# Attention into a mixture of experts: the order of scaling, routing and first expert slices behind the last chunks

## The chip, the cores and the metric

One core of one Trainium2 chip runs the whole kernel. Its engines work side by side, each on its own list of instructions in order: TensorE (PE in the rows; its weight loads are PEld), VectorE (DVE), ScalarE (ACT), GpSimd (POOL) and SyncE (SP, which here only issues DMAs). The metric is the device time of one execution in microseconds (us); less is better.

## The reference

Windowed attention with a linear bias, whose output rows are the tokens of a mixture of experts with one expert per token:

```python
# B, H, S, D = 8, 8, 576, 64; window 128
scores = scale * q @ k^T + slopes * (-|rel|), masked to 0 <= rel < 128
x = softmax(scores) @ v            # -> (4608, 512): N tokens, DM = 512
# E = 8 experts, F = 1024
logits = x @ w_gate
expert_idx = argmax(logits); gate_w = softmax(logits)[expert_idx]
out[mask_e] = gate_w * (relu(x[mask_e] @ w1[e]) @ w2[e])
```

## The kernel before

**Attention** runs over 36 chunks of 128 tokens. For each chunk TensorE makes scores (tile s_ps), VectorE masks them and takes the maximum (nmax), ScalarE takes the exponentials (pe) with their sums, TensorE transposes (t_ps), ScalarE copies the transposes (pT), GpSimd masks them, TensorE multiplies with v (x_ps), and the function rows makes from that the rows in token order, with the gate's logits in 16 more columns of each of four parts: tile r_ps, one buffer in PSUM. VectorE then scales r_ps by 1/sum into x_sb, in two instructions: the logit columns (128x64 elements) and the rows (128x512). The function done, called behind that, sums the logits into lg and has SyncE store the rows to xd in DRAM.

**Routing.** Groups of chunks (GROUPS) go through route, a generator of five stages: one-hot of the chosen expert (oh); rank of each token in its expert, by products with the triangle tri, and the gates; rank within a tile of 128 as a mask lp, and column numbers c; the products rr of an equality mask eq with the token numbers; and the index products lp x rr, added into base, the table from which the rows are gathered later. Rank and index products go into the spare columns of r_ps, from step 146 on into t_ps. route_last does the same for chunk 35 alone, with names that begin with l_, and ends with idx, the table of the first expert's late rows.

**The order is written by hand**: 152 steps, four to a chunk, and each engine's list follows the order in which step calls things. PACE says at which steps a late group takes its next stage. The last full group holds chunks 30 to 34; its first stage runs at step 149, where the rows of chunk 34 are made; those of chunk 35 are made at step 151. To keep TensorE at work, early computes the first layer of seven slices of the first expert for 256 rows that are known by then (e_xh, e_xl to s_ps to e_hh, e_hl; 12 products each, two buffers of s_ps). EP gives the step of each of these slices (0 to 2), LE the slices that route_last puts between its parts (3 to 6). Behind that a scheduler orders the expert layers: first layer2 of the seven early slices, then the rows gathered by idx, and so on.

Of the kernel before, what the change touches and what calls it, by code (L numbers as in the profile page):

```python
# [36 lines left out]
def attention(ctx, tc, st, qT, kT, v, c1, cb, iw, load_c2, chunk_done, chunks, begun):  # L37
# [163 lines left out]
    def rows(ch, subs, xT, rsum):  # L201
        rinv = small.tile([128, H], F32, name="rinv")
        nc.vector.reciprocal(out=rinv, in_=rsum)
        st["r_ps"] = r_ps = ps_r.tile([128, NP, 256], F32, name="r_ps")
        for p in range(NP):
            nc.tensor.matmul(out=r_ps[:, p, 0:XW], lhsT=xT[:, p, :], rhs=iw_sb[:, p, :], start=True, stop=True)  # L206
        x_sb = xp.tile([128, NP, XW], F32, name="x_sb")
        for lo, n in ((128, E), (0, D)):
            cols = slice(lo, lo + 2 * n)
            split = lambda ap: ap[:, :, cols].rearrange("q p (c x) -> q p c x", c=2)  # L210
            nc.vector.tensor_tensor(  # L211
                out=split(x_sb), in0=split(r_ps),
                in1=rinv.rearrange("q (p c) -> q p c", c=2).unsqueeze(3).to_broadcast([128, NP, 2, n]), op=ALU.mult)
        chunk_done(ch, subs, x_sb)
# [54 lines left out]
    def step(s):  # L269
# [21 lines left out]
        if s in EP:  # L291
            early(EP[s])

# [40 lines left out]
LW = (0, 0, 0, 0)  # L334
# [7 lines left out]
EP = {60: "z", 134: "g", 143: "p0", 146: "p1", 147: "0", 149: "1", 150: "2"}  # L342
LE = ("3", "4", "56", "")
# [49 lines left out]
def route(tc, st, lg, c0, G, groups):  # L393
# [65 lines left out]
    for k, n in enumerate(("tokh", "tokl")):  # L459
        nc.vector.tensor_tensor(out=rr[:, :, k, :], in0=eq,  # L460
# [36 lines left out]
def route_last(tc, st, lg, ch, groups):  # L497
# [23 lines left out]
    for r in st["rest"]:  # L521
        next(r)
        next(r)
    st["warm"](1)
# [11 lines left out]
    ip = st["ps_x"].tile([128, 512], F32, name="x_ps")[:, 0:E * TT]
    t0 = EARLY // 128
    for t in range(t0, TT):
        lp = rp.tile([128, 128], BF16, name=f"l_lp{t}", bufs=1)
        nc.vector.tensor_scalar(out=lp, in0=st["i128"], scalar1=s, scalar2=-128.0 * t, op0=ALU.subtract,  # L540
                                op1=ALU.is_equal)
        for k in range(2):
            nc.tensor.matmul(out=ip[:, E * t:E * t + E], lhsT=lp, rhs=rr[:, k, :], start=(k == 0), stop=(k == 1))
# [7 lines left out]
    st["warm"](3)  # L551
# [126 lines left out]
def moe_static(ctx, tc, st, w12, out):  # L678
# [26 lines left out]
    def gather(p, t, behind=None):  # L705
# [7 lines left out]
        else:  # L713
            xg[p, t] = gather_rows(tc, st, g, column(p, t))
# [344 lines left out]
def attn_moe_kernel(ctx, tc, qT, kT, v, c1, cb, c2, iw, w12, out):  # L1059
# [9 lines left out]
    with ExitStack() as actx:  # L1069
# [9 lines left out]
        def done(ch, subs, x_sb):  # L1079
# [7 lines left out]
            for lo in (0, 2):  # L1087
                if lo == 2 and subs[0][0] == subs[2][0]:
                    continue
                n = 64 if subs[0][0] != subs[2][0] else 128  # L1090
                t0 = subs[lo][0] * S + QB * subs[lo][1]
                nc.sync.dma_start(out=st["xd"][t0:t0 + n].rearrange("t (p x) -> t p x", p=NP),
                                  in_=x_sb[QB * lo:QB * lo + n, :, 0:SUB])
# [67 lines left out]
```

## Time and profile before

| | |
|---|---|
| time, median of 3 runs (lowest, highest) | 672.54 us (672.29, 672.86) |
| the profiled execution: its time, its span | 674.61 us, 672.8 us |
| PE busy | 647.7 us (96%) |
| DVE, ACT, POOL busy | 398.6, 313.1, 309.2 us |

The span is the time from the first to the last instruction; 1.8 us lie around it. Busy PE is not PE at its peak, since products overlap and their ends are modelled; what counts here is where it is idle, and what ended that.

### The profile page before, as it was taken

To read this page: it belongs to the slowest core of one execution; us is meant where nothing else is said; L and a number is where in the kernel's file an instruction comes from. 1 tells how busy PE (TensorE), PEld (TensorE's weight loads), DVE (VectorE), ACT (ScalarE), POOL (GpSimd) and SP (SyncE) were. 2 spreads that over 40 slices of the span, in tenths; PEclk is the share of its full clock that TensorE was granted. 3 is DMA by queue.
4 is the path that set the end of the run, shared out by engine and by line. 5 is a ranking of instruction groups with operands and counts; after the bars stand their busy time and mean duration, and the time that the engine had idled before them with its cause. 6 is when DMAs were issued, how large, how long until landed. Compare 5 with 4: busy or idle time off the path is not lost.

```text
span 672.8 us, 15622 instructions
## 1 busy us (share of the span) xinstructions
PE 647.7 (96%) x5937; PEld 551.2 (82%) x5937; DVE 398.6 (59%) x976; ACT 313.1 (47%) x940; POOL 309.2 (46%) x425
## 2 busy tenths in 40 slices
PE   7899999999999989999999999999999999999995
PEld 3688787787787878999988988989898989888884
DVE  3468878877888777553555355365456455456411
ACT  3777778887776511442234234233434333333311
POOL 2546567786654413016524751860762560471202
PEclk8999999999999999999999999999999999999999
DMA  9477696795853316335323442532543542453201
GB/s 319 131 199 182 177 248 164 256 261 133 264 144 82 94 34 189 111 117 170 93 81 109 144 128 82 181 106 85 173 107 109 174 114 77 159 147 111 89 0 59
DMA packets 55360, 94.24 MB, mean 140 GB/s; under 512 B 11622, under 2 KB 31334, under 8 KB 54386
## 3 DMA queue, kind: packets, MB, share of 16 engines
q1 hardware_dynamic: 46882, 73.18, 37.2%
q0 software_dynamic: 8400, 20.02, 10.4%
q8 instruction: 48, 0.79, 0.5%
q14 instruction: 30, 0.25, 0.1%
HBM read 74.20 MB, written 18.97 MB: 138 GB/s over the span
## 4 chain that ended last, share of the span: by engine, by line
PE 51%; issue 8%; POOL 3%; DMA 1%; DVE 1%; ACT 1%; POOLq 0%; ACTq 0%
PE y_ps L762 24%; PE l_ps L634 23%; POOL xg L614 2%; POOL out L749 1%; PE x_ps L762 1%; PE s_ps L634 1%; PE x_ps L596 1%; DMA xd<-x_sb 1%; PE x_ps L196 1%; DMA xg<-xd,idx 0%; PE r_ps L206 0%; DMA out<-y,od_pidx 0%; DVE x_sb L211 0%; ACT pe L159 0%; POOLq L812 0%
## 5 line engine op out<-in xcount | busy, mean ns | idle before, releaser
L637 DVE SCALAR_TENSOR_TENSOR hl<-l_ps,hh 128x334 fp32r<-128x334 f32 (+7 forms) x104 | 52.7, 506 | 162.5 <-ACT hh L636 162.4
L636 ACT ACTIVATE hh<-l_ps 128x334 fp32r<-128x334 f32 (+7 forms) x104 | 46.9, 451 | 216.4 <-PE l_ps L634 216.1
L614 POOL DMA_INDIRECT xg<-xd,od_idx x112 | 114.8, 1025 | 35.8 <-issue 35.2
L159 ACT ACTIVATE pe<-s_ps,nmax 128x128 f32<-128x128 f32 x288 | 102.2, 371 | 48.9 <-DVE nmax L155 39.8
L762 PE MATMUL y_ps<-wh,hh 128*128 128x512 f32 (+2 forms) x288 | 114.2, 397 | 0.0
L762 PE MATMUL y_ps<-wl,hh 128*128 128x512 f32 (+2 forms) x288 | 113.6, 394 | 0.0
L762 PE MATMUL y_ps<-wh,hl 128*128 128x512 f32 (+2 forms) x288 | 113.5, 394 | 0.0
L749 POOL DMA_INDIRECT out<-y,od_pidx x34 | 36.3, 1068 | 153.7 <-ACT y L768 147.2
L852 DVE TENSOR_TENSOR wl<-w_raw,wh 128x512 fp32r<-128x512 f32 x114 | 73.9, 689 | 23.2 <-ACT wh L848 22.1
L634 PE MATMUL l_ps<-xh,wl 128*128 128x304 f32 (+9 forms) x416 | 80.8, 316 | 0.0
L634 PE MATMUL l_ps<-xh,wh 128*128 128x304 f32 (+9 forms) x416 | 80.7, 316 | 0.0
L634 PE MATMUL l_ps<-xl,wh 128*128 128x304 f32 (+9 forms) x416 | 80.6, 316 | 0.0
L634 PEld LDWEIGHTS l_ps<-xh,wh 128*128 128x128 f32 x416 | 68.3, 189 | 7.4
L634 PEld LDWEIGHTS l_ps<-xh,wl 128*128 128x128 f32 x416 | 66.1, 189 | 2.0
L634 PEld LDWEIGHTS l_ps<-xl,wh 128*128 128x128 f32 x416 | 66.0, 189 | 1.9
L196 PE MATMUL x_ps<-pT,v_sb 128*64 128x128 f32 (+2 forms) x1152 | 66.4, 265 | 0.1
L762 PEld LDWEIGHTS y_ps<-wh,hl 128*128 128x128 f32 (+2 forms) x288 | 53.0, 184 | 13.9
L196 PEld LDWEIGHTS x_ps<-pT,v_sb 128*64 128x64 f32 (+1 forms) x1152 | 57.0, 137 | 7.8 <-issue 2.8
L762 PEld LDWEIGHTS y_ps<-wl,hh 128*128 128x128 f32 (+2 forms) x288 | 53.1, 184 | 11.6
L762 PEld LDWEIGHTS y_ps<-wh,hh 128*128 128x128 f32 (+2 forms) x288 | 53.0, 184 | 10.8 <-ACT hh L636 0.4
L159 ACT ACTIVATION_READ_ACCUMULATOR pe<-s_ps,nmax 128x1 f32 x288 | 60.2, 209 | 0.0
L138 PE MATMUL s_ps<-k_sb,q_sb 64*64 64x192 f32 (+2 forms) x1152 | 57.3, 307 | 2.6 <-DMA k_sb<-kT 2.6
(207 smaller groups left out, 980.6 us busy)
## 6 DMA issues: line engine op xcount, KB each, us to landing
w_raw<-w SPq DMA_DIRECT2D x64, 512.0 KB, 3.7
q_sb<-qT SPq DMA_DIRECT2D x40, 256.0 KB, 7.1
xd<-x_sb SPq DMA_DIRECT2D x32, 258.0 KB, 4.9
v_sb<-v SPq DMA_DIRECT2D x32, 256.0 KB, 4.9
k_sb<-kT SPq DMA_DIRECT2D x7, 1152.0 KB, 8.3
xg<-xd,od_idx POOLq DMA_INDIRECT x112, 3.2
xd<-x_sb SPq DMA_DIRECT2D x8, 129.0 KB, 4.2
v_sb<-v SPq DMA_DIRECT2D x8, 128.0 KB, 4.7
```

The source lines that it names most:

```text
L138: nc.tensor.matmul(out=s_ps[halves(a), c, n, x0:x1], lhsT=blocks["q", b, m][h, 2 * g + n, qs], rhs=batch[b][h, 2 * g + n, k0:k0 + x1 - x0] ...
L159: nc.scalar.activation(out=pe[:, h, :], in_=s_ps[:, c, n, lo:lo + 128], func=AF.Exp, bias=nmax[:, 2 * c + n:2 * c + n + 1], scale=1.0, acc ...
L196: nc.tensor.matmul(out=x_ps[64 * c:64 * c + 64, p, q], lhsT=blocks["v", b, m - 1 + kb][0:kk, D * h:D * h + D], rhs=pT[0:kk, kb, h, q], sta ...
L596: nc.tensor.transpose(out=x_ps[:, d, :], in_=g[:, SUB * d:SUB * d + 128], identity=st["ident"])
L614: ins = tc.nc.gpsimd.indirect_dma_start(out=g[:, s], out_offset=None, in_=parts, in_offset=bass.IndirectOffsetOnAxis(ap=idx[:, s], axis=0),)
L634: nc.tensor.matmul(out=ps, lhsT=a[:, 128 * d:128 * d + 128], rhs=b[:, d], start=(k == 0), stop=(k == 11))
L636: nc.scalar.activation(out=hh, in_=ps, func=AF.Relu)
L637: nc.vector.scalar_tensor_tensor(out=hl, in0=ps, scalar=0.0, in1=hh.bitcast(F32), op0=ALU.max, op1=ALU.subtract)
L749: ins = nc.gpsimd.indirect_dma_start(**kw).ins
L762: nc.tensor.matmul(out=ys[t][0:m], lhsT=a[:, tl], rhs=b[:, 512:1024], start=(f == 0 and k == 0), stop=(f == 7 and k == 2))
L852: keep(tc, eng.tensor_tensor(out=wl[:, sl], in0=raw[:, sl], in1=wh.bitcast(F32)[:, sl], op=ALU.subtract))
```

## The change

Five things change.

- The two scalings of a chunk are split: the logit columns are scaled, then lg is summed, then the rows are scaled and stored. For chunks 0 to 33 that is the same place with another order. For chunk 34 scaling and store of the rows wait until the route stage of step 149 is written, for chunk 35 until the rank products of route_last.
- PACE and the step function let a stage be taken twice in a step: the last full group takes two stages at step 150, where it took one, and one in route_last ahead of its index products, where it took two behind the rank.
- Slice 2 moves from step 150 to 149, so that slices 1 and 2 stand in front of the group's rank products. route_last places 3, then 4 and 5, then 6, instead of 3, then 4, then 5 and 6.
- In route_last rank, gate and masks (l_lp) of chunk 35 come first, then the group's fourth stage, then the index products of chunk 35, then those of the group. One of the last full group's two rr products (tokh) moves to GpSimd.
- The gathers of the first expert's late rows and six memsets of hh and hl are held in program order: gathers first.

```diff
@@ rows
-        for lo, n in ((128, E), (0, D)):
+        def scale(lo, n):
...
-        chunk_done(ch, subs, x_sb)
+        scale(128, E)
+        chunk_done(ch, subs, x_sb, lambda: scale(0, D))
@@ step
-            if k[1] <= s and (s in PACE[k[2]] if k[2] in PACE else s % 4 == 2):
+            if k[1] <= s:
                 k[1] = s + 1
-                if next(k[0], k) is k:
-                    st["stages"].remove(k)
+                for _ in range(PACE[k[2]].count(s) if k[2] in PACE else s % 4 == 2):
+                    if next(k[0], k) is k:
+                        st["stages"].remove(k)
+        if "store" in st:
+            st.pop("store")()
@@ tables
-PACE = {21: (122, 126, 130, 132, 134), 27: (138, 142, 144, 146, 148), 30: (149, 150)}
+PACE = {21: (122, 126, 130, 132, 134), 27: (138, 142, 144, 146, 148), 30: (149, 150, 150)}
-EP = {60: "z", 134: "g", 143: "p0", 146: "p1", 147: "0", 149: "1", 150: "2"}
-LE = ("3", "4", "56", "")
+EP = {60: ("z",), 134: ("g",), 143: ("p0",), 146: ("p1",), 147: "0", 149: "12"}
+LE = ("3", "45", "6")
@@ route
-        nc.vector.tensor_tensor(out=rr[:, :, k, :], in0=eq,
+        eng = nc.gpsimd if c0 + G == N // 128 - 1 and k == 0 else nc.vector
+        eng.tensor_tensor(out=rr[:, :, k, :], in0=eq,
@@ route_last
-    for r in st["rest"]:
-        next(r)
-        next(r)
-    st["warm"](1)
+    st.pop("store")()
...
     put_gates(tc, st, gate, groups)
+    t0 = EARLY // 128
+    lps = {}
+    for t in range(t0, TT):
+        lps[t] = rp.tile([128, 128], BF16, name=f"l_lp{t}", bufs=1)
+        nc.vector.tensor_scalar(out=lps[t], in0=st["i128"], scalar1=s, scalar2=-128.0 * t, op0=ALU.subtract,
+                                op1=ALU.is_equal)
+    st["warm"](1)
+    for r in st["rest"]:
+        next(r)
     st["warm"](2)
+    ip = st["ps_x"].tile([128, 512], F32, name="x_ps")[:, 0:E * TT]
+    for t in range(t0, TT):
+        for k in range(2):
+            nc.tensor.matmul(out=ip[:, E * t:E * t + E], lhsT=lps[t], rhs=rr[:, k, :], start=(k == 0), stop=(k == 1))
     for r in st["rest"]:
         list(r)
@@ moe_static
-            xg[p, t] = gather_rows(tc, st, g, column(p, t))
+            xg[p, t] = gather_rows(tc, st, g, column(p, t), held=p == 0)
...
-            nc.gpsimd.memset(a[:, min(CAPS):].bitcast(F32), 0.0)
+            keep(tc, nc.gpsimd.memset(a[:, min(CAPS):].bitcast(F32), 0.0))
@@ done
-            for lo in (0, 2):
...
+            def store():
+                scale()
...
+            if ch < N // 128 - 2:
+                store()
+            else:
+                st["store"] = store
```

VectorE behind the rows of an ordinary chunk, before: both scalings (x_sb), then the sum (lg), then the next scores.

```order
L203 RECIPROCAL rinv<-rsum 128x8
L211 TENSOR_TENSOR x_sb<-r_ps,rinv 128x4x16
L211 TENSOR_TENSOR x_sb<-r_ps,rinv 128x4x128
L1085 TENSOR_REDUCE lg<-x_sb 128x8
L152 COPY_PREDICATED s_ps<-c_sb,s_ps 128x4x128
L155 TENSOR_REDUCE nmax<-s_ps 128x4
```

The same place now:

```order
L203 RECIPROCAL rinv<-rsum 128x8
L212 TENSOR_TENSOR x_sb<-r_ps,rinv 128x4x16
L1095 TENSOR_REDUCE lg<-x_sb 128x8
L212 TENSOR_TENSOR x_sb<-r_ps,rinv 128x4x128
L152 COPY_PREDICATED s_ps<-c_sb,s_ps 128x4x128
L155 TENSOR_REDUCE nmax<-s_ps 128x4
```

The sum stands between the two scalings; so it is at every chunk from 0 to 33.

VectorE at steps 150 and 151, before: the end of the last full group's rank (rank, t), a slice's e_hl, and chunk 35 from 1/sum (rinv) to its one-hot.

```order
L433 TENSOR_REDUCE rank<-pick 128x5
L435 TENSOR_SCALAR t<-rank 128x5
L436 TENSOR_SCALAR t<-t 128x5
L637 SCALAR_TENSOR_TENSOR e_hl<-s_ps,e_hh 128x256
L203 RECIPROCAL rinv<-rsum 128x8
L211 TENSOR_TENSOR x_sb<-r_ps,rinv 128x4x16
L211 TENSOR_TENSOR x_sb<-r_ps,rinv 128x4x128
L1085 TENSOR_REDUCE lg<-x_sb 128x8
L503 CAST l_prev<-run 128x8
L505 TENSOR_REDUCE l_mx<-lg 128x1
L507 SCALAR_TENSOR_TENSOR l_key<-lg,l_mx,c_sb 128x8
L508 TENSOR_SCALAR l_mx<-l_mx 128x1
```

The same place now:

```order
L439 TENSOR_REDUCE rank<-pick 128x5
L441 TENSOR_SCALAR t<-rank 128x5
L442 TENSOR_SCALAR t<-t 128x5
L450 SCALAR_TENSOR_TENSOR p<-t,rank 128x5
L452 TENSOR_TENSOR lp<-c_sb,p 128x640
L455 TENSOR_SCALAR c<-mk 128x5
L457 TENSOR_SCALAR big<-rank 128x5
L203 RECIPROCAL rinv<-rsum 128x8
L212 TENSOR_TENSOR x_sb<-r_ps,rinv 128x4x16
L1095 TENSOR_REDUCE lg<-x_sb 128x8
L510 CAST l_prev<-run 128x8
L512 TENSOR_REDUCE l_mx<-lg 128x1
```

The group's third stage (p, lp, c, big) stands ahead of chunk 35's scaling, the slice's e_hl has gone ahead of the rank, and the scaling of chunk 35's rows behind its one-hot.

TensorE at steps 149 and 150, before: slice 1 (with the numbers that tell the slices apart), then the rank of the last full group.

```order
L634 MATMUL s_ps_4430<-e_xh_68,wh_1983 128x256 x4
L634 MATMUL s_ps_4430<-e_xh_68,wl_1984 128x256 x4
L634 MATMUL s_ps_4430<-e_xl_69,wh_1983 128x256 x4
L419 LDWEIGHTS tri_148
L419 MATMUL t_ps_4447<-oh_4426,tri_148 128x40
```

The same place now:

```order
L644 MATMUL s_ps_4430<-e_xh_68,wh_1983 128x256 x4
L644 MATMUL s_ps_4430<-e_xh_68,wl_1984 128x256 x4
L644 MATMUL s_ps_4430<-e_xl_69,wh_1983 128x256 x4
L644 MATMUL s_ps_4447<-e_xh_68,wh_2218 128x256 x4
L644 MATMUL s_ps_4447<-e_xh_68,wl_2219 128x256 x4
L644 MATMUL s_ps_4447<-e_xl_69,wh_2218 128x256 x4
L425 LDWEIGHTS tri_148
L425 MATMUL t_ps_4464<-oh_4424,tri_148 128x40
```

Slice 2 stands between slice 1 and the rank.

## Rows read from the trace of the kernel before

**Rows 1.** Busy time of each engine in two stretches, with the number of instructions, the granted TensorE clock, the DMA share and GB/s: the change from attention to the experts (235 to 262 us), and the expert layers behind it.

```profile
235.00:262.00 27.00, 23.86 (x173) 20.67 (x172) 19.66 (x98) 5.03 (x14) 7.90 (x13) 1.00 0.36 105
...
262.00:640.00 378.00, 378.00 (x2067) 333.74 (x2067) 197.17 (x425) 133.50 (x212) 160.76 (x178) 1.00 0.40 121
```

**Rows 2.** TensorE in order of time at four of the products that write into the spare columns of r_ps (start us, length us, line, operation; in brackets the idle time before it and what ended it).

```profile
62.85 0.18 PE L419 MATMUL r_ps<-oh,tri 128*128 128x40 bf16 x1 [0.41 <-DVE x_sb L211]
...
81.14 0.41 PE L466 MATMUL r_ps<-rr,lp 128*128 128x48 bf16 x10 [0.88 <-DVE x_sb L211]
...
211.16 0.46 PE L466 MATMUL r_ps<-rr,lp 128*128 128x48 bf16 x12 [1.18 <-DVE x_sb L211]
...
222.24 0.17 PE L419 MATMUL r_ps<-oh,tri 128*128 128x24 bf16 x1
```

**Rows 3.** VectorE in order of time at the third of these: the two scalings of a chunk (merged in one row), the sum of its logits, and the next instruction.

```profile
210.28 0.82 DVE L211 TENSOR_TENSOR x_sb<-r_ps,rinv 128x64 f32<-128x64 f32 x2
211.02 0.26 DVE L1085 TENSOR_REDUCE lg<-x_sb 128x8 f32<-128x64 f32 x1
211.19 0.69 DVE L152 COPY_PREDICATED s_ps<-c_sb,s_ps 128x512 f32<-128x512 uint32 x1
```

**Rows 4.** VectorE, instructions grouped by line and shape: busy us in all, mean ns of one.

```profile
L211 DVE TENSOR_TENSOR x_sb<-r_ps,rinv 128x512 f32<-128x512 f32 x36 | 24.5, 680 | 0.0
...
L211 DVE TENSOR_TENSOR x_sb<-r_ps,rinv 128x64 f32<-128x64 f32 x36 | 8.1, 225 | 4.5 <-PE r_ps L206 1.5
```

**Rows 5.** VectorE and TensorE in order of time, rows with idle time in front of them: where VectorE waited for the score products, and TensorE for the copies of the transposed weights.

```profile
84.53 0.43 DVE L152 COPY_PREDICATED s_ps<-c_sb,s_ps 128x256 f32<-128x256 uint32 x1 [1.83 <-PE s_ps L138]
...
130.40 0.70 DVE L152 COPY_PREDICATED s_ps<-c_sb,s_ps 128x512 f32<-128x512 uint32 x1 [0.38 <-PE s_ps L138]
...
166.96 0.70 DVE L152 COPY_PREDICATED s_ps<-c_sb,s_ps 128x512 f32<-128x512 uint32 x1 [0.33 <-PE s_ps L138]
...
213.86 0.70 DVE L152 COPY_PREDICATED s_ps<-c_sb,s_ps 128x512 f32<-128x512 uint32 x1 [0.94 <-PE s_ps L138]
...
226.83 0.66 PE L168 MATMUL t_ps<-c_sb,pe 128*128 128x128 f32 x4 [0.44 <-ACT pT L170]
```

**Rows 6.** TensorE in order of time, 237 to 255 us: products of ranks (L419, L519), slices of the first expert layer (L634), products with the second layer (L762), index products (L466), transposes of gathered rows (L596).

```profile
237.96 0.18 PE L419 MATMUL t_ps<-oh,tri 128*128 128x40 bf16 x1 [0.84 <-DVE oh L413]
...
238.17 0.72 PE L634 MATMUL s_ps<-e_xh,wh 128*128 128x256 f32 x4
...
239.68 1.14 PE L206 MATMUL r_ps<-iw_sb,xT 128*128 128x144 f32 x8
...
242.89 0.17 PE L519 MATMUL x_ps<-l_oh,tri 128*128 128x8 bf16 x1 [0.64 <-DVE l_oh L515]
...
246.60 0.75 PE L634 MATMUL s_ps<-e_xh,wh 128*128 128x256 f32 x4 [0.57 <-DVE e_hl L637]
...
249.45 0.47 PE L762 MATMUL y_ps<-wh,e_hh 128*128 128x512 f32 x1 [0.87 <-DVE base L468]
...
250.63 0.48 PE L762 MATMUL y_ps<-wh,e_hh 128*128 128x512 f32 x1
...
250.94 0.39 PE L762 MATMUL y_ps<-wl,e_hh 128*128 128x512 f32 x1
...
251.17 0.40 PE L762 MATMUL y_ps<-wh,e_hl 128*128 128x512 f32 x1
...
254.67 0.66 PE L596 MATMUL x_ps<-c_sb,xg 128*128 128x128 f32 x4 [0.21 <-DMA xg<-xd,idx]
```

**Rows 7.** VectorE in order of time, 235 to 245 us.

```profile
235.73 0.82 DVE L211 TENSOR_TENSOR x_sb<-r_ps,rinv 128x64 f32<-128x64 f32 x2 [0.75 <-PE r_ps L206]
...
236.78 0.20 DVE L402 TENSOR_REDUCE mx<-lg 128x5 f32<-128x40 f32 x1
...
238.35 0.20 DVE L425 TENSOR_TENSOR pick<-t_ps,oh 128x40 f32<-128x40 f32 x1
...
240.29 0.42 DVE L637 SCALAR_TENSOR_TENSOR e_hl<-s_ps,e_hh 128x256 fp32r<-128x256 f32 x1 [0.39 <-ACT e_hh L636]
...
240.63 0.19 DVE L203 RECIPROCAL rinv<-rsum 128x8 f32<-128x8 f32 x1
...
242.61 0.23 DVE L515 TENSOR_SCALAR l_oh<-l_key,mk 128x8 bf16<-128x8 f32 x1
...
243.51 0.16 DVE L444 SCALAR_TENSOR_TENSOR p<-t,rank 128x5 f32<-128x5 f32 x1
...
244.64 0.17 DVE L453 TENSOR_TENSOR c<-c,t 128x5 f32<-128x5 f32 x1
```

**Rows 8.** Instructions grouped by line and shape: a product of two tiles on GpSimd, and on VectorE the one of two that the change moves to GpSimd (busy us in all, mean ns of one).

```profile
L869 POOL TENSOR_TENSOR wl<-w_raw,wh 128x512 fp32r<-128x512 f32 x14 | 18.5, 1322 | 3.5 <-ACT wh L864 3.4
...
L460 DVE TENSOR_TENSOR rr<-eq,c_sb 128x240 bf16<-128x240 f32 x8 | 3.2, 442 | 0.1
```

**Rows 9.** DMA issues from the page: tiles, queue, operation, number, KB in all, median us from issue to landing.

```profile
xd<-x_sb SPq DMA_DIRECT2D x32, 258.0 KB, 4.9
```

**Rows 10.** TensorE at the wait near the start, and busy time of each engine in two stretches behind it, with the granted clock (columns as in Rows 1).

```profile
8.19 0.67 PE L138 MATMUL s_ps<-k_sb,q_sb 64*64 64x64 f32 x16 [2.56 <-DMA k_sb<-kT]
...
9.00:10.00 1.00, 0.94 (x10) 0.17 (x12) 0.96 (x2) 0.00 (x0) 0.17 (x1) 0.50 1.07 382
...
12.00:13.00 1.00, 1.00 (x21) 0.71 (x24) 0.59 (x1) 0.31 (x2) 0.00 (x0) 0.81 1.11 446
```

More of the change, by code (lines that the diff above doesn't have):

```diff
@@ L290, in step @@
             st["load"]((s - FETCH + 12) // 8)
-        if s in EP:
-            early(EP[s])
+        for op in EP.get(s, ()):
+            early(op)
     with tc.manual_schedule(engines=HANDS(nc)):
@@ L333 @@
 RB = 2
-LW = (0, 0, 0, 0)
+LW = (0, 0, 0)
 FREE_T = 146
 WU = (9, 1, 1, 1, 1, 1, 2, 2, 2, 2, 2, 1, 0)
-PACE = {21: (122, 126, 130, 132, 134), 27: (138, 142, 144, 146, 148), 30: (149, 150)}
+PACE = {21: (122, 126, 130, 132, 134), 27: (138, 142, 144, 146, 148), 30: (149, 150, 150)}
 GROUPS = ((0, 5), (5, 5), (10, 5), (15, 6), (21, 6), (27, 3), (30, 5), (35, 1))
@@ L532, in route_last @@
     put_gates(tc, st, gate, groups)
+    t0 = EARLY // 128
[7 more added lines that the diff above has]
+        next(r)
     st["warm"](2)
+    ip = st["ps_x"].tile([128, 512], F32, name="x_ps")[:, 0:E * TT]
+    for t in range(t0, TT):
+        for k in range(2):
+            nc.tensor.matmul(out=ip[:, E * t:E * t + E], lhsT=lps[t], rhs=rr[:, k, :], start=(k == 0), stop=(k == 1))
     for r in st["rest"]:
         list(r)
[L536 to L543, printed above, removed]
     v = lambda ap: ap.rearrange("p (e t) -> p t e", t=TT)
@@ L550, in route_last @@
     nc.vector.tensor_tensor(out=run[:, ch + 1, :], in0=run[:, ch, :], in1=oh, op=ALU.add)
-    st["warm"](3)
 def slots(tc, st, pool, e, s0):
@@ L583, with gather_rows @@
 CONSTS = (("ident", 128), ("seq", MAXOV), ("rev", E), ("prof", E), ("tokh", N // 128), ("tokl", N // 128), ("i128", 128), ("grp", 1))
-def gather_rows(tc, st, g, idx, n=N + 1, **kw):
-    tc.nc.gpsimd.indirect_dma_start(
+def gather_rows(tc, st, g, idx, n=N + 1, held=False, **kw):
+    ins = tc.nc.gpsimd.indirect_dma_start(
         out=g, out_offset=None, in_=st["xd"][0:n, :], in_offset=bass.IndirectOffsetOnAxis(ap=idx, axis=0), **kw
     )
+    if held:
+        keep(tc, ins)
     return g
@@ L1077, in begun, with done @@
                     keep(tc, nc.vector.tensor_copy(out=st["hl"][:, :, j], in_=st[n]))
-        def done(ch, subs, x_sb):
+        def done(ch, subs, x_sb, scale):
             c0, G = next((c, n) for c, n in GROUPS if c <= ch < c + n)
@@ L1086, in done @@
                                     axis=AX.XY, op=ALU.add)
-            for lo in (0, 2):
[L1088 to L1093, printed above, removed]
+            def store():
+                scale()
+                for lo in (0, 2):
+                    if lo == 2 and subs[0][0] == subs[2][0]:
+                        continue
+                    n = 64 if subs[0][0] != subs[2][0] else 128
+                    t0 = subs[lo][0] * S + QB * subs[lo][1]
+                    nc.sync.dma_start(out=st["xd"][t0:t0 + n].rearrange("t (p x) -> t p x", p=NP),
+                                      in_=x_sb[QB * lo:QB * lo + n, :, 0:SUB])
+            if ch < N // 128 - 2:
+                store()
+            else:
+                st["store"] = store
             if g == G - 1:
```

## Prediction

> **What bounds the kernel now.** I read the busy time by stage first [rows 1]. From 262 us to 640 us TensorE has no idle time, and its list of work there stays as it is, so whatever TensorE is late at 262 us comes out at the end, one for one, and the only question is how its idle time before that changes. From 235 to 262 us it is busy 23.86 of 27 us; the 3.13 us of idle time stand in front of five instructions [rows 6]: 0.84 before the last full group's rank (waits for VectorE's one-hot), 0.64 before chunk 35's rank (the same), 0.57 before a slice (for e_hl), 0.87 before the first second-layer product (for base), 0.21 before the first gathered rows. The change aims at these. But its first part acts in all of attention, so I read next what TensorE waits for there. Products of the routing that write into r_ps wait until VectorE has finished scaling the rows of the same r_ps [rows 2]: at 211.16 the product starts 0.06 behind the end of that scaling at 211.10 [rows 3]. Nine products stand so, each 0.05 or 0.06 behind the scaling; the first and the last are the ones at 62.85 and 222.24.
>
> **Part 1, the scalings split by the sum.** Before, the rows' scaling starts 0.14 behind the logits' (0.82 for both less 0.68 [rows 3, 4]), the sum 0.74 behind it. Now the sum must wait for the logits' scaling: 0.225 [rows 4] and a step of 0.03, which is what dependent VectorE instructions show here (mx at 236.78 lasts 0.20, and its reader starts at 237.01). So the sum starts at 0.255; the rows' scaling follows as the next instruction did behind the sum, 0.17 later (211.02 to 211.19), at 0.43, and ends at 0.43 + 0.68 = 1.11 instead of 0.82: **0.29 later**. The next instruction starts 0.60 behind it (0.74 - 0.14), at 1.03, against 0.74 + 0.17 = 0.91: VectorE is 0.12 longer per chunk, for one more dependent step that is not hidden.
>
> So each of the nine products comes 0.29 later, if VectorE was on time before it. Is that given back? VectorE catches up soon after each and waits for TensorE's scores again, as at 84.53 (1.83 us) and 213.86 (0.94) [rows 5]; ScalarE waits for VectorE's maxima, and TensorE's later waits for the transposes' copies start from those same scores. All engines move together, so I carry the delay on. Two products get more and two less. At 141.97 and 179.65 VectorE has not waited since 130.40 and 166.96 [rows 5], with one more chunk in between, so its own 0.12 comes on top: 0.41. At 211.16 its lateness since the preceding wait at 202.82 is in already, and 0.12 is new; at 222.24 the 0.29 meets a wait of 0.44 at 226.83 [rows 5], where only VectorE's 0.12 counts. Sum: 5 x 0.29 + 2 x 0.41 + 2 x 0.12 = 2.51, less some 0.06 at two places where TensorE itself arrived late: **+2.45**. Bounds: with the sum's 0.17 alone, 9 x 0.17 = 1.5, and 0.3 of it absorbed, 1.2; with 9 x 0.29 and three times 0.12, 3.0.
>
> The Trainium skill's page VectorE: DVE Perf Modes (The DRAIN you can't avoid) says that a semaphore between two VectorE operations costs nothing extra, since the pipeline empties either way. By that the dependent step would be free and the delay 0.17 a product, some 674.3 us in all. The trace disagrees: the independent sum starts at 211.02, 0.08 ahead of the scaling's end at 211.10, where a dependent one starts 0.03 behind the end.
>
> **Part 2, the front of the transition.** Chunk 34's sum starts 0.49 earlier (0.255 against 0.74), and so does all up to the group's one-hot. With slice 2 in front of the rank, TensorE doesn't wait: the 0.84 goes, and with it 0.17 of a slice's tail. Behind the rank r_ps of chunk 35 starts at 239.68 - 1.01 = 238.67, and r_ps is free by then: VectorE's scaling of chunk 34's rows is done by 238.1. What is late next is VectorE. Slice 2's e_hl now stands in front of the group's rank sums (pick). Before, e_hl started 0.61 behind the slice's last issue (239.68 to 240.29 [rows 6, 7]). A slice takes 1.51 (238.17 to 239.68) and slice 2 now issues until 238.46, so e_hl starts at 239.07, and pick 0.34 later at 239.41, where it stood at 238.35. From pick VectorE was through at 239.90 (240.29 less its idle 0.39): 1.55. Then comes the stage that is taken early, 1.13 (243.51 to 244.64), and 0.03, so chunk 35's 1/sum starts at 242.12 instead of 240.63. From there to the one-hot it was 1.98 (to 242.61), now 0.49 less: 243.61, and the rank on TensorE 0.28 later, **243.89 instead of 242.89**. TensorE, after slice 3, has nothing from 241.23 on: one wait of 2.66 us takes the place of the 0.84 and 0.64.
>
> **Part 3, behind the last one-hot.** VectorE has less left, since the third stage is done. Slices 4 and 5 run from 243.95 to 246.97, slice 6 at once behind them (its buffer is freed by slice 4's e_hl at about 246.95, so the 0.57 goes), until 248.51; rank, gate and the four masks lie beside them. Slice 5's e_hl starts at 246.97 + 0.61 = 247.58, column numbers and eq take until 248.77. Then tokh runs on GpSimd. The trace has no such shape there; 128x512 takes 1.32 [rows 8], 240 of 512 elements 0.62, plus a step: 0.67, to 249.45. The bounds are VectorE's 0.44 for the same product [rows 8] and the whole 1.32. The group's ten index products, 0.42 to 0.45 long, then base and the first second-layer product at about 250.32, where it was 249.45. Before, eight mask products stood among the first three of these: 249.45 to 250.63 is 1.18, three alone are 3 x 0.23 [rows 6], so 0.48 was theirs; now they run while TensorE waits for GpSimd. The fourth such product thus starts at 251.0 instead of 250.63, **+0.4**. idx is ready some 0.6 earlier than it was, so the gather is earlier and the wait of 0.21 at 254.67 goes: **+0.2** for the whole transition. Range of it: -0.8 (VectorE's steps half a microsecond quicker, GpSimd as VectorE) to +1.2 (GpSimd at 1.32, and a third of a microsecond in steps between engines).
>
> **Costed at nothing.** The six memsets behind the gathers run while GpSimd waits for the next table; without that cover they would be 2 us in front of a gather. Chunk 35's store leaves at 245.25 instead of 241.76 and lands 4.9 later [rows 9], at 250.2, with the gather at about 250.5; it may take 6.2 before TensorE notices. The stores and the gates keep their order on SyncE's queue, and nothing else is moved past them.
>
> **The sum.** 2.45 + 0.2 = +2.65 us on the profiled execution's 674.61 (its span 672.8 and 1.8 around it), 677.3. That execution lies 2.07 above the median of 672.54, so the predicted median is **675.2**. About 0.2%, 1.35 us, is what a measurement here can tell from no change.
>
> **Rivals.**
> - *The clock falls, 676.8.* At 8.19 TensorE had waited 2.56 us, and from 9 to 12 us the granted clock was 0.50, 1.2 of 2.4 GHz, and 0.81 in the stretch behind [rows 10]. The new wait of 2.66 is as long. Some 3.2 us at half speed are 1.6 us of work: +1.6. Against it: the wait is framed by dense slices, where that one had little work before it. [...]
> - *Attention absorbs its delay, 673.1.* TensorE's next wait for a transposes' copy, 0.44 at 226.83, is longer than 0.29. If such waits swallow the delays, VectorE's 0.12 at two or three products and the +0.2 remain, +0.6. Against it: these waits hang on TensorE's own scores.
> - *The lead is kept, faster, 670.9.* TensorE is 1.01 ahead at r_ps of chunk 35. If VectorE reaches the last one-hot a microsecond earlier than I count, at 242.9 or before, the lead lasts; with the 0.21 and 0.4 of the waits for base that is -1.6, if attention costs nothing as well. Against it: the stage of 1.13 in front of the one-hot is certain.
>
> **How the numbers follow.** Forecast 0.52 (a twelfth of it under +1.35), clock 0.15, absorbed 0.20, lead kept 0.13 (a little of it within 0.2%). Slower 0.48 + 0.15 = 0.63; same 0.04 + 0.20 + 0.02 = 0.26; faster 0.11. The range leaves out the faster case and the top of the clock case: 672.0 to 677.2. The forecast alone, 1.2 - 0.8 to 3.0 + 1.2, is 672.9 to 676.7.
>
> **What would show it.** In the changed profile: the rows' scaling ends 1.11 behind the start of the logits' scaling, and the products of rows 2 wait for it 0.3 longer; TensorE stands 2.4 us later at the group's rank; the wait before that rank is gone, and one of 2.7 stands before chunk 35's; the clock is 1.00 or not behind it. Wrong would be: a one-hot of chunk 35 that comes no later than TensorE, or index waits that don't grow.

## The result and the profile after

| | before | after |
|---|---|---|
| time, median (lowest, highest) | 672.64 us (672.29, 672.86) | 679.1 us (678.14, 679.59) |
| ratio, 95% interval | | 1.0088 (1.0075 to 1.0102): +5.9 us |
| profiled execution: span | 672.8 us | 676.4 us |

Slower, as forecast, but 5.9 us by the ratio (6.5 by the medians) and not 2.65: 679.1 us lies above the range of 672.0 to 677.2. The spans shown differ by less than the times for two reasons. The execution profiled after was the fastest of its four. And the one before had lost time at its start: its 2.56 us for k [rows 10] were 1.5 after. So I count stretches from the same transposes' wait near 30 us in each profile: 31.24 before, 29.80 after. By that the rows of chunk 34 (r_ps) start 3.2 us later after the change, and the first second-layer product 5.5 (253.51 less 29.80, against 249.45 [rows 6] less 31.24).

What TensorE waited for after the change: the sum in us, the number of waits and the longest (left out are two rows of the start and one of 0.2):

```profile
PE t_ps L168 <- ACT pT L170: 5.9, 11, 1.0
PE r_ps L473 <- DVE x_sb L212: 4.6, 5, 1.4
PE x_ps L526 <- DVE l_oh L522: 2.6, 1, 2.6
PE r_ps L425 <- DVE x_sb L212: 2.0, 3, 0.9
...
PE t_ps L473 <- POOL rr L467: 0.9, 1, 0.9
PE x_ps L606 <- DVE xl L608: 0.7, 1, 0.7
PE r_ps L483 <- DVE x_sb L212: 0.5, 1, 0.5
PE y_ps L772 <- DVE base L475: 0.4, 1, 0.4
```

The three rows on x_sb are attention's: 7.1 us, where before they were 3.7. The waits for pT are attention's too (5.9, before 6.4). The others stand behind attention. TensorE in order of time from the rows of chunk 34 on:

```profile
236.21 1.23 PE L206 MATMUL r_ps<-iw_sb,xT 128*128 128x144 f32 x8
...
240.13 0.19 PE L425 MATMUL t_ps<-oh,tri 128*128 128x40 bf16 x1
...
245.53 0.17 PE L526 MATMUL x_ps<-l_oh,tri 128*128 128x8 bf16 x1 [2.59 <-DVE l_oh L522]
...
247.41 1.05 PE L644 MATMUL s_ps<-e_xh,wh 128*128 128x256 f32 x4
...
252.71 0.41 PE L473 MATMUL t_ps<-rr,lp 128*128 128x48 bf16 x10 [0.91 <-POOL rr L467]
...
253.51 0.47 PE L772 MATMUL y_ps<-wh,e_hh 128*128 128x512 f32 x1 [0.39 <-DVE base L475]
...
260.96 0.66 PE L606 MATMUL x_ps<-c_sb,xg 128*128 128x128 f32 x4 [0.67 <-DVE xl L608]
...
266.48 0.70 PE L644 MATMUL l_ps<-xh,wh 128*128 128x292 f32 x4
```

No wait is left before the group's rank, and one of 2.59 stands before chunk 35's: that was forecast (2.66). New are the waits for GpSimd's product (0.91) and for xl (0.67), and slices whose groups of four products last 1.05 instead of 0.64; the wait for base was 0.87 and is 0.39. The last line is the first product of the rows gathered by idx (l_ps); it serves below as a mark. Stretches of the same execution (columns as in Rows 1):

```profile
235.00:246.00 11.00, 8.41 (x91) 8.09 (x86) 7.47 (x38) 2.49 (x8) 0.00 (x0) 1.00 0.21 51
246.00:247.00 1.00, 1.00 (x10) 1.00 (x9) 1.00 (x5) 0.28 (x1) 0.00 (x0) 0.83 0.03 8
247.00:250.00 3.00, 3.00 (x16) 3.00 (x16) 1.51 (x10) 0.38 (x1) 0.00 (x0) 0.50 0.30 88
250.00:251.00 1.00, 1.00 (x10) 1.00 (x10) 0.37 (x2) 0.38 (x1) 0.00 (x0) 0.97 0.00 0
```

From 247 to 250 us the granted clock is 0.50, 1.2 GHz: slice 5 takes 2.56 us (247.41 to 249.97) where one takes 1.51. The fall came behind the wait of 2.59 and about 1 us of slice 4's work. From 262 us on TensorE is busy throughout in both, so all that differs lies ahead of that.

### The profile page after: what moved, and what is told of

Read it like the earlier page. It is cut to its first block, busy times and chain, and to the rows that moved or that the text cites. A ratio compares the mean times of both kernels' runs of the same rounds, so it can differ in the third digit from the quotient of the medians.

```text
span 676.4 us, 15619 instructions
## 1 busy us (share of the span) xinstructions
PE 648.3 (96%) x5937; PEld 552.4 (82%) x5937; DVE 403.1 (60%) x975; ACT 313.9 (46%) x940; POOL 310.8 (46%) x426
## 4 chain that ended last, share of the span: by engine, by line
PE 49%; issue 8%; POOL 3%; DMA 1%; DVE 1%; POOLq 0%; ACT 0%; ACTq 0%; SPq 0%
PE y_ps L772 24%; PE l_ps L644 23%; POOL xg L624 2%; POOL out L759 1%; PE x_ps L772 1%; DMA xd<-x_sb 1%; PE x_ps L606 1%; DMA out<-y,od_pidx 0%; DMA xd<-gate 0%; DVE od_pos_u L1005 0%; POOLq L822 0%; POOL pace L717 0%; DVE x_sb L212 0%; PE l_ps L616 0%; DVE xl L608 0%
## 5 line engine op out<-in xcount | busy, mean ns | idle before, releaser
L858 ACT CAST wh<-w_raw 128x1024 fp32r<-128x1024 f32 x57 | 59.5, 1044 | 0.0
```

The costliest lines, as they stand in the source:

```text
L858: keep(tc, nc.scalar.copy(out=wh, in_=raw))
```

## The experiments

The kernel before ran beside each, on the same chip; its median lay between 672.96 and 675.40 on the chips used, so only ratios are compared between groups. 0.001 is 0.67 us. "Mean clock" is the granted clock over a whole execution.

### Attention: the split

**e1**, the kernel before once more. 

> The kernel before, unchanged, to see its span from run to run. In its profile TensorE's first score product waited 2.56 us for the k DMA, in the changed kernel's profile 1.53. If that start is what made the profiled execution 2.07 us longer than the median, this profile has a shorter wait there and a span near 671. If the profile is simply longer than an unprofiled execution, the wait may be anything and the profiled time stays about 2 us above the median of 672.6.

Measured 1.0003 (0.9992 to 1.0014). Its profiled execution spans 670.7 us with 0.51 us of wait for k, as the first of the two cases had it.

**e2**, the split alone: the sum between the scalings in all 36 chunks.

```diff
-        for lo, n in ((128, E), (0, D)):
...
-        chunk_done(ch, subs, x_sb)
+        scale(128, E)
+        chunk_done(ch, subs, x_sb, lambda: scale(0, D))
...
+            scale()
```

> Before, with only the sum of the logits put between the two scalings, at all 36 chunks. Carried-delay theory: nine products into r_ps come 0.29 later each and TensorE is 3.2 us late at chunk 34's rows, as in the changed kernel when the start is taken off: +2.5 to +3.5 us on the median, less 0.5 at the last chunks where the logits come earlier. Absorption theory: at most +0.9 us. If the difference of the medians (6.5) that the profiles don't show (5.0) comes from attention, this costs over 4.

**e3**, the change with the old scalings for chunks 0 to 33.

```diff
+        if ch < N // 128 - 2:
+            scale(0, D)
-        chunk_done(ch, subs, x_sb, lambda: scale(0, D))
+        chunk_done(ch, subs, x_sb, lambda: ch < N // 128 - 2 or scale(0, D))
```

> The changed kernel with the rows scaled ahead of the sum again for chunks 0 to 33, so that what is left of the change is the order behind attention. Carried-delay theory: 3.2 us of the 6.5 go, +2.2 to +3.3 is left (the wait of 2.6 before the last chunk's rank, the half clock behind it, GpSimd's product). Absorption theory: the scaling costs under 0.9, and +5.5 or more is left. Prediction's count of the transition: +0.2, or +1.8 with the half clock.

e2 measured 1.0055 (1.0042 to 1.0068), 3.7 us, and its waits on x_sb are those of the changed kernel; e3 measured 1.0033 (1.0018 to 1.0048), 2.2 us. 0.0055 and 0.0033 add up to the whole 0.0088. So the delay of the products is carried on, and the rival that attention absorbs it falls.

**e13**, the split at 24 chunks, without the twelve whose rows stand directly ahead of a routing product into r_ps.

```diff
+        whole = ch in (5, 8, 10, 13, 15, 18, 21, 24, 27, 28, 29, 31)
+        if whole:
+            scale(0, D)
+        chunk_done(ch, subs, x_sb, lambda: whole or scale(0, D))
```

> The kernel before, with the sum between the scalings at 24 chunks only: the twelve whose rows stand directly ahead of a routing product into r_ps (5, 8, 10, 13, 15, 18, 21, 24, 27, 28, 29, 31) keep the old order. Theory one, that the cost in attention is TensorE's wait for the rows' scaling at those products: the waits stay at 0.41, 0.88, 0.43, 0.59, 0.18 and 1.18, and the time within 0.3 us of before, ratio 1.0000 to 1.0005. Theory two, that VectorE's longer list (0.12 per chunk) is what costs: 24 x 0.12 = 2.9, ratio 1.004.

Measured 1.0005 (0.9991 to 1.0019). The products of the routing in it, as in [rows 2]:

```profile
61.72 0.18 PE L425 MATMUL r_ps<-oh,tri 128*128 128x40 bf16 x1 [0.41 <-DVE x_sb L212]
...
210.51 0.46 PE L472 MATMUL r_ps<-rr,lp 128*128 128x48 bf16 x12 [1.18 <-DVE x_sb L212]
...
222.95 0.18 PE L425 MATMUL r_ps<-oh,tri 128*128 128x24 bf16 x1
```

The waits of these products are those of before, with one new one of 0.43 at 91.89. That one isn't the split's: e18, which splits none of the first 34 chunks, has the same 0.43 at 91.36. VectorE's longer list costs nothing that can be measured (the interval reaches from -0.6 to +1.3 us); the twelve chunks carry the rest.

One more wait in this profile has nothing to do with the split. At 221.36 TensorE waits 1.29 for a copy of transposes, where before it waited 0.22. All profiles from e5 to e18 have it (1.29 to 1.32, with either order of scaling), none of the six before them has it. With it TensorE comes about 1.5 us later to chunk 34's rows (203.15 us behind the wait near 30 us in e3, 204.73 in e16, both with the old scalings). What causes it isn't known, so spans of the two groups can't be set against each other.

**e14 and e15**, the routing products in t_ps from the start (`FREE_T = 0`), in e2 and in the kernel before.

> The kernel with the split alone (e2, ratio 1.0055), but the routing products write into t_ps from the start, so that none of them shares r_ps with the scaling. Theory one: the waits on x_sb go, 7.1 us of them in e2; in their place come waits around t_ps, whose one buffer the transposes need, of unknown size; what counts is the difference to the run with the old order and t_ps, which should be under 0.5 us. Theory two (VectorE's list): the difference to that run stays near 3.7 us.

> The kernel before, with the routing products in t_ps from the start: the partner of the run before this. The waits on x_sb (3.7 us) go. If the waits for t_ps are shorter than those, it is faster than the kernel before by up to 3 us, ratio 0.996 to 1.000; if the one buffer of t_ps holds up the transposes at each stage, slower by some us.

e14 measured 1.0124 (1.0100 to 1.0148), e15 1.0119 (1.0094 to 1.0144), medians 684.02 and 682.79 us. No product waits for x_sb in either; eleven wait for the copies out of t_ps instead (12.9 us in e15), which is dearer. With the shared tile gone the split costs 0.3 us by the ratios and 1.2 by the medians, not 3.7; the intervals are too wide to say which.

### Behind attention: the long wait and the clock

**e4**, the changed kernel with slice 4 ahead of the last rank.

```diff
-LE = ("3", "45", "6")
+LE = ("34", "5", "6")
```

> The changed kernel with slice 4 moved ahead of the last chunk's rank, into the wait of 2.59 us that stands there. If that wait is worth its length, 1.5 us of it fill and the clock stays at 1.00: -2.0 to -2.8 us against the changed kernel. If VectorE is the bound of the whole transition, TensorE only waits elsewhere (for the product on GpSimd, for base): under -1.0, and what is gained is the half clock.

Measured 1.0060 (1.0047 to 1.0074), 1.9 us less than the change. The 2.59 is 1.16 and 0.56 now, and the clock is 1.00 behind it. But the wait for GpSimd is 0.95, and a new one of 1.01 stands before the gathered rows.

**e8 and e16**, ten products of a zero tile in the wait (`LW = (10, 0, 0)`), in the changed kernel and in e3.

> The changed kernel with ten products of a zero tile (128x512, not part of the result) between slice 3 and the last rank, in the wait of 2.59, which they nearly fill. If the half clock behind that wait (0.50 from 247 to 250 us in the profile) is met in most executions, the clock stays at 1.00 and the time falls by 1 us, ratio 1.0073 against 1.0088; if it is met in few, the time stays within 0.3 us; if the products run over, it grows by what they run over, at most 0.5.

> The kernel of e3 (ratio 1.0033, mean clock 0.991 to 0.997) with ten products of a zero tile (not part of the result) in the wait before the last rank, as e8 had them in the changed kernel. If what those won there (0.0020 of the time) was the half clock, it is won here too: ratio 1.0013, with a mean clock of 0.997 in most executions. If it was something of that chip, the ratio stays at 1.003.

e8 measured 1.0068 (1.0056 to 1.0081), 0.0020 under the change; e16 1.0014 (0.9999 to 1.0029), 0.0019 under e3. TensorE in e8, and the stretch that had the half clock:

```profile
243.59 2.33 PE L89 MATMUL x_ps<-warm 128*128 128x512 bf16 x10
246.33 0.18 PE L526 MATMUL x_ps<-l_oh,tri 128*128 128x8 bf16 x1 [0.41 <-DVE l_oh L522]
```

```profile
247.00:250.00 3.00, 3.00 (x27) 2.89 (x26) 2.36 (x14) 0.85 (x3) 0.00 (x0) 1.00 0.31 91
```

The products do nothing for the result, leave the other waits of the transition about as they were (0.74, 0.39, 0.64), and win 1.3 us by either pair of ratios. Each difference is uncertain by more than 1 us, and in e8 some of it may be attention's: its profile has the wait of 1.29 near 222 us, and the last of the nine products, which waits 0.91 in the changed kernel, doesn't wait there. The profiles give the price without that. From chunk 34's rows to the first product of the gathered rows (l_ps), before the change and in e8:

```profile
234.47 1.23 PE L206 MATMUL r_ps<-iw_sb,xT 128*128 128x144 f32 x8
...
262.51 0.70 PE L634 MATMUL l_ps<-xh,wh 128*128 128x292 f32 x4
```

```profile
237.02 1.23 PE L206 MATMUL r_ps<-iw_sb,xT 128*128 128x144 f32 x8
...
265.96 0.70 PE L644 MATMUL l_ps<-xh,wh 128*128 128x292 f32 x4
```

That is 28.04 us before, 28.94 in e8 (28.95 in e16), and 30.27 in the changed kernel (236.21 to 266.48), the only one of these with the half clock in this stretch: 1.3 us for the clock, 0.9 for the waits.

The mean clock tells less. It is 0.997 or more in five of e8's six executions and 0.993 to 0.996 in all four of the changed kernel, but executions of the kernel before reach from 0.993 to 0.999 as well, since the start lowers it too. In e3, with its wait of 2.59, it is 0.997 in the two shortest executions (spans 670.9 and 671.0), 0.991 or 0.992 in four of the longest five (674.1 to 675.1) and 0.944 in the fifth. So the fall isn't met in every execution; these differ by 3 to 4 us, more than the 1.3, so the clock behind this wait isn't all that sets them apart.

**e9**, e3 and e4 together. 

> The changed kernel with the old scalings for chunks 0 to 33 (as e3) and slice 4 between slice 3 and the last rank (as e4), so that no wait there is longer than 1.2 us. If the cost of attention, the half clock behind the long wait and the waits of the transition add up, 1.0060 (e4) less 0.0055 (e2) is left: ratio 1.0005 to 1.0012, with a mean clock as in the kernel before (0.997); waits of 1.16 before the last rank, 0.56, 0.95, 0.39 and about 1.0 for the gathered rows. If they overlap, so that only one of the two savings counts, ratio 1.003.

Measured 1.0014 (1.0002 to 1.0026), waits 1.16, 0.56, 0.40, 0.39, then 0.61 and 0.63 for the gathered rows. The savings add up, less some half clock: its profile has 0.57 from 244 to 248, with no longer wait than e4 had.

### Behind attention: what else was moved

**e5**, e3 with chunk 35's rows scaled and stored at once.

```diff
-            if ch < N // 128 - 2:
+            if ch != N // 128 - 2:
                 store()
...
-    st.pop("store")()
```

> The kernel with the old scalings of the run before (e3, ratio 1.0033, waits of 2.59 before the last rank, 0.70 for GpSimd's product, 0.39 for base, 0.40 and 0.77 for the gathered rows), but chunk 35's rows are scaled and stored at once behind its sum, ahead of its one-hot. Theory one, that the last gate's store waits for the landing of chunk 35's rows and the gather waits for that gate: the gate then finds the rows landed, the gather goes as soon as idx is ready, the two waits of 1.17 for the gathered rows go down to 0.2 or less; the wait before the last rank grows by the scaling, 0.6, to 3.2; about -0.4 us in all, ratio 1.0027. Theory two, that the gathered rows wait for something else (the table idx, the queue): the two waits stay, and only the 0.6 is added, ratio 1.0042.

**e10**, the same edit in e9. 

> The kernel of e9, with chunk 35's rows scaled and stored at once behind its sum (as e5, now without the long wait and its half clock). Theory one, the gather held by the gate and the gate by the rows' store: the gate's store leaves before 248 us, the gather goes when idx is ready, the wait of 1.0 for gathered rows falls to 0.3 or less, the wait before the last rank grows from 1.16 to 1.8; -0.1 us against e9. Theory two: the wait for gathered rows stays and 0.6 is added.

e5 measured 1.0046 (1.0033 to 1.0059), e10 1.0020 (1.0007 to 1.0033) against e9's 1.0014. In both the last rank waits longer by 0.54 (3.13, 1.70), as expected, and no wait for the gathered DMA is left. The stores on SyncE's queue (start, length of the issue) and the first gather on GpSimd's, in e3 and then in e10:

```profile
243.68 0.55 SPq L1107 DMA_DIRECT2D xd<-x_sb  x1
247.91 0.33 SPq L503 DMA_DIRECT2D xd<-gate  x1
...
250.40 0.98 POOL L597 DMA_INDIRECT xg<-xd,idx  x1 [2.44 <-DVE runb L992]
```

```profile
243.91 0.54 SPq L1106 DMA_DIRECT2D xd<-x_sb  x1
247.56 0.33 SPq L503 DMA_DIRECT2D xd<-gate  x1
...
252.46 0.99 POOL L596 DMA_INDIRECT xg<-xd,idx  x1 [1.70 <-DVE runb L991]
```

In e3 idx is done at 249.00 and the gather starts 1.4 later, 2.49 behind the gate's issue, although the row names runb. The same 2.49 or 2.50 stands in e4, e7, e8, e9 and e16. The gate's store in turn leaves 3.6 to 4.3 behind the rows' store, though in e3 the gates were ready at 244.25. What SyncE's queue waited for there:

```profile
SPq L503 <- DMA xd<-x_sb: 3.6, 1, 3.6
```

The program asks for this order: the store of the rows writes all 516 columns of a row of xd, and the gate goes into the last of them. In e10 the gather starts 4.90 behind the gate and 0.67 behind idx (251.79): the chain of store, gate and gather has let go. But a wait of 0.68 for xl (VectorE) appears in its place, so the time is not better.

**e6**, e3 with the group's third stage behind chunk 35's masks again; **e7**, e3 with both token products on VectorE.

```diff
-PACE = {..., 30: (149, 150, 150)}
+PACE = {..., 30: (149, 150)}
     for r in st["rest"]:
         next(r)
+        next(r)
```

> The kernel of e3, but the last full group's third stage (p, lp, c, big; 1.13 us on VectorE) stands again behind chunk 35's masks, together with the fourth. Theory one, that the new wait before the last rank is VectorE's third stage: 2.59 becomes 1.46, and the 1.13 comes back in front of the group's products, so that the wait for GpSimd's product grows from 0.70 to 1.8; what is won is only that the last gate's store leaves 1.1 earlier, so that the waits for gathered rows (1.17) shrink by up to 1.1: -0.3 to -1.1 us, ratio 1.0017 to 1.0029. Theory two, that the early stage costs nothing since VectorE had time there: the 2.59 stays, and the time grows by 1.1, ratio 1.005.

> The kernel of e3, but both products of the last full group with the token numbers stand on VectorE, as before the change. If GpSimd's 0.81 is the cost, the wait before the group's index products falls from 0.70 to 0.25. Theory one, with the gather held by the gate's store: the 0.45 comes back as longer waits for the gathered rows (1.17 to about 1.6), and the time stays, ratio 1.0033. Theory two, without that chain: -0.45 us, ratio 1.0026. Such a difference is at the edge of what the times tell, the waits in the profile decide.

e6 measured 1.0038 (1.0022 to 1.0054). Its waits are as expected: 2.59 became 1.37, 0.70 became 1.87. What the earlier gate won was lost at the clock, 0.58 from 252 to 256 us behind the 1.87. e7 measured 1.0035 (1.0023 to 1.0047): 0.70 became 0.28, and 0.40 became 0.62 before the gathered rows. Nothing is gained, as theory one had it for e7.

**e11**, e10 with both of these edits. 

> The kernel of e10, with the group's third stage again behind chunk 35's masks and both token products on VectorE: of the change there remain slices 1 and 2 ahead of the group's rank, slices 3 and 4 ahead of chunk 35's, and chunk 35's rank, gate and masks ahead of the rest of the group. If VectorE's chain to base sets the end of this stretch, the wait before the last rank falls to about 0.7 and that before the index products takes over what was won, 1 us or more; ratio 1.0000 to 1.0010. If the order itself is good and only the early stage, GpSimd's product and the late store spoilt it, it is faster than the kernel before by 0.5 to 1 us, ratio 0.9985 to 0.9993.

Measured 1.0019 (1.0005 to 1.0032): waits of 0.49, 0.56, 1.61, 0.39, 0.66. What goes before the last rank comes back before the index products; the order itself isn't better.

**e12**, the kernel before with slice 2 ahead of the group's rank (`149: "12"`). 

> The kernel before, with slice 2 ahead of the group's rank and nothing else of the change. Theory one, that slice 2's e_hl, now in front of the rank's sums on VectorE, hands the wait on: the 0.84 before the group's rank goes, the one-hot of chunk 35 comes some 0.5 later, the wait before the last rank grows from 0.64 to about 2.0; +0.3 to +0.5 us, ratio 1.0005 to 1.0007, and possibly a half clock. Theory two, that a wait filled is a wait won: -0.84 us, ratio 0.9988.

Measured 1.0011 (0.9997 to 1.0025): the 0.84 is gone, and the 0.64 is 1.84. The wait filled here was handed on, and grew: 1.48 us in two waits became 1.84 in one. The time itself can't be told from no change.

**e17 and e18**, the kernel before with the rows of chunks 34 and 35 (e18: of 34 alone) scaled and stored late, as in the change.

> The kernel before, with one part of the change: for chunks 34 and 35 alone the sum stands ahead of the rows' scaling, and scaling and store of the rows wait until the group's first stage and chunk 35's rank are written; slices, stages and GpSimd as before. Theory: the group's one-hot comes 0.49 earlier, chunk 35's by another 0.6, so the waits of 0.84 and 0.64 fall to about 0.35 and 0; the last gate's store, held by the later store of chunk 35's rows, leaves about 1 us later, which the gather just allows (gate plus 2.49 against idx). Of the 1.1 some comes back as longer waits for e_hl and base (0.57 and 0.87 before): 0.3 to 1.1 us faster, ratio 0.9984 to 0.9996. Rival: VectorE's chain to base has the same length as before, all of it comes back, ratio 1.0000; or the gate's chain reaches the gathered rows, slower by up to 1 us.

> The kernel of the run before with chunk 34 alone; chunk 35's rows are scaled and stored as before, so the last gate's store is not held. Theory: the wait of 0.84 falls to 0.35, and since chunk 35's one-hot comes earlier by as much, the 0.64 stays; -0.2 to -0.5 us, ratio 0.9993 to 0.9997. Rival: the 0.49 comes back in front of base, ratio 1.0000.

e17 measured 0.9997 (0.9983 to 1.0010), e18 1.0003 (0.9990 to 1.0015). The waits of e17:

```profile
237.69 0.18 PE L428 MATMUL t_ps<-oh,tri 128*128 128x40 bf16 x1 [0.37 <-DVE oh L422]
242.15 0.17 PE L528 MATMUL x_ps<-l_oh,tri 128*128 128x8 bf16 x1 [0.19 <-DVE l_oh L524]
246.46 0.74 PE L645 MATMUL s_ps<-e_xh,wh 128*128 128x256 f32 x4 [1.17 <-DVE e_hl L648]
249.28 0.47 PE L773 MATMUL y_ps<-wh,e_hh 128*128 128x512 f32 x1 [0.87 <-DVE base L477]
```

0.84 and 0.64 [rows 6] fell to 0.37 and 0.19 (forecast 0.35 and 0), and 0.57 grew to 1.17: of 0.92 won, 0.32 is left, too little to measure. In e18 the 0.84 fell to 0.36 and the 0.64 stayed (0.66), as forecast; a gain of half a microsecond would not show in its time either. No version tried is measurably faster than the kernel before.

## Why the prediction was wrong

The 5.9 us split into three parts, against a forecast of 2.45 + 0.2: attention 3.7 (e2), the half clock 1.3 (e8 and e16), the waits of the transition 0.9 (e16's 0.0014, which has neither of the others). As ratios each is uncertain by about a microsecond, and e16's interval reaches no change. The profiles, without the ratios, give 3.2, 1.3 and 0.9.

**Attention: right mechanism, one product mis-sized.** Nine products wait longer for the scaling, and with the split kept away from them (e13) no cost can be measured. Eight of the nine grew by 0.24 to 0.37, near the 0.29 of the forecast, 2.5 in all. The step that failed is "at 222.24 the 0.29 meets a wait of 0.44 at 226.83, where only VectorE's 0.12 counts". In the changed kernel:

```profile
223.89 0.17 PE L425 MATMUL r_ps<-oh,tri 128*128 128x24 bf16 x1 [0.91 <-DVE x_sb L212]
...
228.27 0.66 PE L168 MATMUL t_ps<-c_sb,pe 128*128 128x128 f32 x4 [0.23 <-ACT pT L170]
```

That product waits 0.91 (0.91 and 0.92 in e2 and e4), and the wait behind it shrank only from 0.44 to 0.23: 0.7 in place of 0.12. That makes 2.5 + 0.9 - 0.2 = 3.2, the delay seen at the rows of chunk 34; e2's interval begins at 2.8. Why 0.91? VectorE in order of time before that product, sh and oh before the change and then the same stretch in the changed kernel, with GpSimd beside it:

```profile
218.39 0.18 DVE L404 TENSOR_TENSOR sh<-lg,mx 128x24 f32<-128x24 f32 x1
...
219.42 0.34 DVE L413 TENSOR_TENSOR oh<-key,mk 128x24 bf16<-128x24 f32 x1
```

```profile
219.20 0.61 DVE L410 TENSOR_TENSOR sh<-lg,mx 128x24 f32<-128x24 f32 x1
219.85 0.56 DVE L412 SCALAR_TENSOR_TENSOR key<-sh,c_sb 128x24 f32<-128x24 f32 x1
220.44 0.18 DVE L417 TENSOR_REDUCE mk<-key 128x3 f32<-128x24 f32 x1
220.65 0.46 DVE L419 TENSOR_TENSOR oh<-key,mk 128x24 bf16<-128x24 f32 x1
```

```profile
219.14 0.63 POOL L180 TENSOR_SCALAR_AFFINE_SELECT pT<-pT 128x512 f32<-128x512 f32 x1
219.74 0.64 POOL L178 TENSOR_SCALAR_AFFINE_SELECT pT<-pT 128x512 f32<-128x512 f32 x1
220.44 0.63 POOL L180 TENSOR_SCALAR_AFFINE_SELECT pT<-pT 128x512 f32<-128x512 f32 x1
```

Now each of sh, key and oh starts while a mask select runs and ends 0.03 to 0.04 behind its end. Before, sh fell where one select followed another; sh and oh together are 0.55 longer now. With the 0.29 that is 0.84 of the 0.91. The Trainium skill's page SBUF — State Buffer (SBUF: two separate sides) says that a VectorE operation with two inputs in SBUF and a GpSimd operation that reads SBUF lock one port pair against each other, and that the one that starts first keeps it for its whole instruction. These rows agree, and mk, a reduction with one input, keeps its 0.18. So a delay of 0.3 on VectorE moved two short instructions under GpSimd's, and the forecast, which shifted all engines together, could not have that. No run moved the selects alone: this cause of the 0.91 is read from the rows, not shown.

**The clock: a rival that came true beside the forecast.** Its mechanism and price were named (1.6 us; 1.3 measured), but it was taken as an alternative with a chance of 0.15, on "the wait is framed by dense slices", and so stood outside the sum. That is the second step that failed. The half clock had followed a wait of that length near the start [rows 10], which was the better witness for the changed kernel's profile; but e3 and e7 have the same 2.59 and no fall in theirs. So neither argument decided the case, and the forecast should have carried part of the price.

**The transition: a wait moves, as forecast; one cost of nothing was wrong.** The 2.59 came as worked out. From chunk 34's rows to chunk 35's rank it took 9.32 us (forecast 9.42), from there to the first second-layer product 6.50 in e8 and 6.47 in e3, both at full clock (forecast 6.43). The missing 0.7 of 0.9 against 0.2 lies behind that, in a wait for xl or the gathered rows that was put at nothing. And e6, e11 and e12 show that VectorE's work from the group's one-hot to base sets the length: what is taken from one wait comes back in a later one.

- GpSimd's token product took 0.81, not 0.62, and TensorE's index products wait 0.91 for it (0.74 in e8 at full clock); the term of 0.67 was too small by 0.2. By luck most of it was hidden: eq was through 0.1 to 0.15 earlier than forecast (e8, e3).
- "Costed at nothing: the six memsets behind the gathers". The wait of 0.67 for xl points to them. The cast ahead of xl before the change, VectorE there in the changed kernel, and the first and last of the memsets:

```profile
254.69 0.17 DVE L995 CAST od_pos_u<-od_pos 128x8 uint32<-128x8 f32 x1
```

```profile
258.26 1.47 DVE L1005 CAST od_pos_u<-od_pos 128x8 uint32<-128x8 f32 x1
...
259.81 0.50 DVE L1015 TENSOR_REDUCE od_idx<-od_pick 128x42 f32<-128x336 f32 x1
260.23 0.68 DVE L608 TENSOR_TENSOR xl<-x_ps,xh 128x512 fp32r<-128x512 f32 x1
```

```profile
257.86 0.37 POOL L791 MEMSET hh<- 128x306 f32 x1
...
259.32 0.37 POOL L791 MEMSET hl<- 128x306 f32 x1
```

  A cast of 8 columns lasts until the memsets are through (259.69) and xl comes behind it. In nine profiles (the changed kernel, e3, e5, e7 to e11 and e16) the cast ends 0.02 to 0.04 behind the last memset, and TensorE waits 0.63 to 0.77 for xl. Where the cast doesn't meet the memsets, it takes 0.17: they run ahead of the gathers before the change and in e1, it is through before them in e4 and comes behind them in e6. I asked only whether GpSimd was idle there, not whom its work holds up. No run put the memsets back alone, and in e3, e7 and e9 the cast starts 0.35 to 0.53 ahead of the first memset and is held all the same, so the cause is argued, not shown.
- "Costed at nothing: chunk 35's store". I asked when its rows land for the gather; the gate's store, queued behind and into a column that the rows' store writes too, waits for that landing, and the gather for the gate. In the changed kernel's profile, with its half clock, idx was later still (253.69, where the gate would have let the gather go at 253.20). In e3, e4, e7 and e9 the chain decides when the gather starts, and TensorE waits 0.40 to 1.01 for the gathered rows.

**Rivals.** Absorption fell with e2. The lead kept fell with the changed kernel's own profile, where chunk 35's one-hot came as late as forecast; e12 and e11 say the same of the order. The clock came, on top.

## What to carry to other kernels

When a write into a shared PSUM tile waits for the last reader, every instruction put ahead of that reader is paid at each such write: split only where nothing waits behind (24 chunks took it here for nothing that could be measured; with the other 12 it cost 3.7 us). A step that fills one wait of TensorE gains only if it also shortens the other engine's chain to the last thing TensorE needs; look for that chain first, and count what its new longest wait does to the clock. For a store that is moved, follow the later stores into the same rows and their readers; for work moved to or on GpSimd, ask what VectorE does beside it.

## What was not expected of the hardware

- No length of wait told whether the clock would fall. Profiles with a fall: 2.59 (changed kernel), 3.13 (e5), 1.87 (e6), 1.70 (e10), 1.16 followed by 0.56 (e9). Without: 2.59 (e3 and e7), 1.84 (e12), 1.16 followed by 0.56 (e4). What decides stays open.
- The same TensorE wait for a copy of transposes (near 221 us, later in e14 and e15) was 0.21 or 0.22 in six profiles and 1.29 to 1.32 in fourteen, whatever the edit.
- VectorE instructions of 0.17 to 0.2 us lasted 0.61 (sh) and 1.47 (the cast) beside GpSimd's; what holds the cast isn't shown.
